# Attention followed by a gated FFN on one core: even 512-column blocks, weights by cast DMA, preps per row, attention a block ahead

## The chip, the cores and the metric

The kernel runs on one core of a Trainium2 chip. The metric is device time in microseconds (us) for one execution; the time before is 392.04 us, the median of three runs (389.96 to 392.66). Engines are named as the profile names them: PE is TensorE's matmul stream and PEld its weight loads, DVE is VectorE, ACT is ScalarE, POOL is GpSimd, and SP is SyncE, which only issues transfers here.

## The reference

The inputs are q, k and v of shape (8 batches, 8 heads, 576 rows, 64), and three FFN weights of shapes 512 x 1536 (gate), 512 x 1536 (value) and 1536 x 512 (out), all float32. The output is 4608 x 512 float32.

```
theta = pi/2 * arange(S) / S                       # S = 576
phi(x) = concat([relu(x) * cos(theta), relu(x) * sin(theta)], axis=-1)
kv  = einsum('bhsf,bhsd->bhfd', phi(k), v)
z   = sum(phi(k), axis=rows)
att = einsum('bhsf,bhfd->bhsd', phi(q), kv) / (phi(q) . z + 1e-6)
x   = att with heads side by side, reshaped to (4608, 512)
out = (gelu(x @ w_gate) * (x @ w_val)) @ w_out
```

So each batch needs two products whose inner size is small (kv with 65 columns, the last being z; nm, the numerator and the denominator), and then every row passes through three dense products, which are most of the arithmetic.

## The kernel before

Everything runs on one core, in an order that is written out by hand: `tc.manual_schedule()` keeps each engine's instructions in the order in which the code names them, and the framework only adds the waits. A loop such as "for jt in range(JT)" below is therefore an order on five queues at once. An instruction that waits holds back everything behind it on its engine.

**Layout.** The 8 heads are 4 pairs (`pair`, NP = 4); a pair fills 128 partitions, 64 per head, and each partition holds R = 9 consecutive rows of 64 values. The 4608 tokens are columns of `xT`; the FFN works on blocks of BLK = 512 columns (9 blocks), while a batch has 576 columns, so batch and block boundaries drift apart. JT = 12 is the number of 128-wide slices of the hidden size 1536; a pass over `jt` for one block is called a block here, and one `jt` of it a slot.

**Attention of one batch.** `prep` (L151) makes qp and kp: per pair and for cosine and sine, one DVE instruction over 128 x 576 values with two tensor sources, the data and the broadcast table. `cast_v` (L187) makes the bfloat16 copy of v with the column of ones, on POOL. `kv_unit` (L237, L245) runs 72 small matmuls and two ACT copies. `turn_q` (L220) turns qp into qT with two DMA transposes on SP; `turn_q_pe` (L205, L212) does it for batch 0 with TensorE transposes and ACT copies. `nm_unit` (L260, L271 to L273) takes 128 columns of qT at a time, five steps per batch (NT = 5): eight matmuls, then three DVE instructions (den, rec, x). `xt_unit` (L309, L317) turns x and ACT copies it into `xT`.

**FFN of one block.** `gv_unit` (L332, L340, L345) does one slot: four matmuls for the gate and four for the value into one PSUM tile `gv_ps` (two buffers), gelu on ACT, the product hT on DVE. A slot's `gv_ps` is free for the slot after next when its hT is done. `o_part` (L370, L379) does the out product of 128 rows; in the steady state a third of it, four matmuls, stands in each slot, for the block before. `flush` (L359) stores the finished rows from SP.

**Loads.** All loads are issued by SP. The weights come in float32 through a staging pool of four buffers in four column slices (L90, L101), and ACT (L96) and POOL (L97, L105) cast them. q, k and v come as two halves per batch and tensor (L71), with three buffers each.

**Order.** Batch 0's loads, then the first two weight slices; batch 0's preps, spread over DVE, ACT (`prep_act`, L166) and POOL (`prep_pool`, L178, L179); kv, then `attend_burst(0)`: all five nm/xt steps with nothing between. Then the gates of batch 0's 576 columns as two halves of 288, with batch 1's preps in the last slots; then kv and the burst of batch 1; then the out product of block 0 by itself; then the segment of 448 columns that completes block 1, in which batch 2's preps, transposes, kv and nm/xt steps are woven; then blocks 2 to 8. In block i, for i from 2 to 6, batch i + 1 is attended: q preps in slots 0 and 1, the transposes and k preps from slot 2, kv in slot 5, nm from slot 6. Blocks 7 and 8 have no attention. The tail is the out product of block 8.

Of the kernel before, what the change touches and what calls it, by code (L numbers as in the profile page):

```python
# [9 lines left out]
FP32 = mybir.dt.float32  # L10
# [6 lines left out]
def kernel(  # L17
# [31 lines left out]
    wst = ctx.enter_context(tc.tile_pool(name="wst", bufs=4))  # L49
    inp = ctx.enter_context(tc.tile_pool(name="inp", bufs=3))  # L50
# [15 lines left out]
    def load(name, src, b, half, pieces=1):  # L66
        t = inp.tile([128, 2, R * D], FP32, name=name)
        view = rows(src, b)
        step = 2 // pieces
        for m in range(0, 2, step):  # L70
            nc.sync.dma_start(  # L71
                out=t[:, m:m + step], in_=view[:, 2 * half + m:2 * half + m + step]
            )
        staged[name, b, half] = t
# [7 lines left out]
    W_SLICES = [(0, 3), (3, 3), (6, 3), (9, 3)]  # L82
    wstage = {}

    def load_w(i):
        jt0, n = W_SLICES[i]
        sl = slice(jt0 * 128, (jt0 + n) * 128)
        for name, src in (("wgf", wg_r), ("wvf", wv_r)):
            t = wst.tile([128, CT, 384], FP32, name=name, tag="w")
            nc.sync.dma_start(out=t[:, :, 0:n * 128], in_=src[:, :, sl])  # L90
            wstage[name, i] = t

    def cast_w(i):
        jt0, n = W_SLICES[i]
        sl = slice(jt0 * 128, (jt0 + n) * 128)
        nc.scalar.copy(wg_sb[:, :, sl], wstage["wgf", i][:, :, 0:n * 128])  # L96
        nc.gpsimd.tensor_copy(wv_sb[:, :, sl], wstage["wvf", i][:, :, 0:n * 128])  # L97

    def load_wo(i):
        t = wst.tile([128, 3, C], FP32, name="wof", tag="w")  # L100
        nc.sync.dma_start(out=t, in_=wo_r[:, 3 * i:3 * i + 3])  # L101
        wstage["wof", i] = t

    def cast_wo(i):
        nc.gpsimd.tensor_copy(wo_sb[:, 3 * i:3 * i + 3], wstage["wof", i])  # L105


    for half in range(2):
        load("qf", q, 0, half, pieces=2)
    for half in range(2):  # L110
        load("kf", k, 0, half, pieces=2)
        load("vf", v, 0, half, pieces=2)
# [33 lines left out]
    def prep(name, b, pair, part, n=1):  # L146
        dst = phi_tile(name, b)
        src = staged[name[0] + "f", b, pair // 2]
        tab = (cos_t, sin_t)[part]
        for m in range(pair, pair + n):  # L150
            nc.vector.scalar_tensor_tensor(  # L151
                dst[:, m, :, part * D:(part + 1) * D],
                src[:, m % 2].rearrange("p (j d) -> p j d", j=R),
                0.0,
                tab[:, :, None].to_broadcast([128, R, D]),
                op0=ALU.max,
                op1=ALU.mult,
            )

    def prep_act(name, b, half, part):  # L160

        dst = phi_tile(name, b)
        src = staged[name[0] + "f", b, half].rearrange("p m (j d) -> p m j d", j=R)
        tab = (cos_t, sin_t)[part]
        for j in range(R):
            nc.scalar.activation(  # L166
                dst[:, 2 * half:2 * half + 2, j, part * D:(part + 1) * D],
                src[:, :, j],
                AF.Relu,
                scale=tab[:, j:j + 1],  # L170
            )

    def prep_pool(name, b, half, part):
        dst = phi_tile(name, b)
# [6 lines left out]
            pos,  # L181
            tab[:, None, :, None].to_broadcast([128, 2, R, D]),
            op=ALU.mult,
        )

    def cast_v(b, half, copy=nc.gpsimd.tensor_copy):
        copy(  # L187
# [335 lines left out]
```

## Time and profile before

| | us |
|---|---|
| median of the runs shown (3) | 392.04 |
| the profiled execution, its own time | 394.85 |
| span of that execution in the trace | 392.7 |

| stage | from | to | length |
|---|---|---|---|
| loads, preps, kv and burst of batch 0 | 0 | 26.4 | 26.4 |
| gates of batch 0, 2 x 288 columns, 12 slots | 26.4 | 62.4 | 36.0 |
| kv and burst of batch 1 | 62.4 | 76.0 | 13.6 |
| out product of block 0 | 76.0 | 88.4 | 12.4 |
| gates of 448 columns, attention of batch 2 | 88.4 | 125.6 | 37.2 |
| blocks 2 to 6, attention of batches 3 to 7 | 125.6 | 315.8 | 190.2 |
| blocks 7 and 8 | 315.8 | 378.0 | 62.2 |
| out product of block 8, last stores | 378.0 | 392.7 | 14.7 |

All times of stages and rows below are those of the one profiled execution, counted from the start of its span; that execution took 0.7% longer than the median. A row of the profile names the line of the code, the engine, the operation, what it writes and reads, and in brackets how long the engine stood idle before it and who released it. "PEclk" is the clock that TensorE was granted, as a share of full speed.

### The profile page before, as it was taken

The numbers are of one execution on the slowest core, as the hardware profiler recorded it, in microseconds if no ns is written. First come the engines' busy times: TensorE is split into PE (matmuls) and PEld (weight loads), VectorE is DVE, ScalarE is ACT, GpSimd is POOL, SyncE is SP. The second block draws the span as 40 slices with busy tenths as digits, with TensorE's granted clock in tenths as the row PEclk, the third lists the DMA queues.
The fourth block names the chain that finished last, engine by engine and source line by source line (L and its number), as shares of the span: only waits on it lengthen the run. The fifth ranks groups of instructions, "written<-read, shape, count | busy, mean of one in ns | idle before, by whom it ended". The sixth has DMA issues, their size and how long they took to land.

```text
span 392.7 us, 6081 instructions
## 1 busy us (share of the span) xinstructions
PE 342.5 (87%) x2484; PEld 177.1 (45%) x2484; DVE 204.6 (52%) x379; ACT 128.7 (33%) x242; POOL 36.8 (9%) x35
## 2 busy tenths in 40 slices
PE   2588955899576988998999999979997999999995
PEld 2365633544243444544544454535443544444442
DVE  6653496504945873587449556915693522222210
ACT  5755421213123331433333242314232333223321
POOL 1821530000202000200020011002000000000000
PEclk9999986599888998999999999989999999999999
DMA  8989908029495099309933990597056111111214
GB/s 265 381 278 362 388 15 120 2 66 357 65 222 214 2 142 321 128 1 126 340 126 44 192 350 6 86 246 258 2 84 118 29 27 42 40 27 28 52 42 95
DMA packets 57467, 55.83 MB, mean 142 GB/s; under 512 B 34912, under 2 KB 39008, under 8 KB 57440
## 3 DMA queue, kind: packets, MB, share of 16 engines
q1 hardware_dynamic: 57440, 55.45, 51.7%
q8 instruction: 19, 0.31, 0.3%
q14 instruction: 8, 0.07, 0.0%
HBM read 37.75 MB, written 9.44 MB: 120 GB/s over the span
## 4 chain that ended last, share of the span: by engine, by line
PE 71%; DMA 14%; DVE 8%; ACT 3%; POOL 2%; issue 1%; ACTq 0%; DVEq 0%; POOLq 0%
PE gv_ps L332 41%; PE o_ps L370 17%; PE gv_ps L370 6%; DVE qp L151 4%; PE xt L309 3%; PE nm L260 3%; DMA qT_1449<-qp 2%; DMA qT_3175<-qp 2%; DMA qT_2744<-qp 2%; DMA qT_1113<-qp 2%; DMA qT_702<-qp 2%; DMA qT_1881<-qp 2%; DVE hT L345 2%; DMA qT_2312<-qp 2%; DVE x_sb L273 1%; POOL pos L178 1%
## 5 line engine op out<-in xcount | busy, mean ns | idle before, releaser
L345 DVE TENSOR_TENSOR hT<-gel,gv_ps 128x512 bf16<-128x512 f32 (+2 forms) x132 | 76.0, 589 | 152.2 <-ACT gel L340 152.0
L340 ACT ACTIVATE gel<-gv_ps 128x512 f32<-128x512 f32 (+2 forms) x120 | 66.5, 555 | 203.9 <-PE gv_ps L332 203.0
L332 PE MATMUL gv_ps<-xT,wg_sb 128*128 128x512 bf16 x336 | 88.7, 388 | 0.0
L332 PE MATMUL gv_ps<-xT,wv_sb 128*128 128x512 bf16 x336 | 87.5, 383 | 0.0
L370 PE MATMUL o_ps<-wo_sb,hT 128*128 128x512 bf16 x336 | 87.1, 382 | 0.0
L332 PEld LDWEIGHTS <-wg_sb 128*128 128x128 bf16 x480 | 47.6, 101 | 64.0 <-issue 18.0
L332 PEld LDWEIGHTS <-wv_sb 128*128 128x128 bf16 x480 | 48.6, 101 | 49.9 <-issue 4.2
L370 PEld LDWEIGHTS <-hT 128*128 128x128 bf16 x432 | 41.2, 100 | 44.7 <-issue 3.5
L332 PE MATMUL gv_ps<-xT_335,wg_sb 128*128 128x288 bf16 (+1 forms) x144 | 30.0, 335 | 11.2 <-DVE hT L345 10.9
L332 PE MATMUL gv_ps<-xT_335,wv_sb 128*128 128x288 bf16 (+1 forms) x144 | 30.3, 339 | 0.0
L151 DVE SCALAR_TENSOR_TENSOR qp<-qf,cos_t 128x576 bf16<-128x576 f32 x32 | 26.0, 849 | 2.5 <-DMA qf<-in_q_dram 2.4
L151 DVE SCALAR_TENSOR_TENSOR kp<-kf,cos_t 128x576 bf16<-128x576 f32 x32 | 25.9, 851 | 1.5 <-DMA kf<-in_k_dram 1.5
L273 DVE TENSOR_TENSOR x_sb<-nm,rec 128x512 bf16<-128x512 f32 x34 | 23.5, 692 | 1.2
L370 PE MATMUL gv_ps<-wo_sb,hT 128*128 128x512 bf16 x96 | 23.3, 407 | 0.0
L151 DVE SCALAR_TENSOR_TENSOR kp<-kf,sin_t 128x576 bf16<-128x576 f32 x30 | 22.3, 788 | 0.0
L151 DVE SCALAR_TENSOR_TENSOR qp<-qf,sin_t 128x576 bf16<-128x576 f32 x30 | 21.4, 752 | 0.0
L309 PE MATMUL xt<-ident,x_sb 128*128 128x128 bf16 x144 | 15.6, 238 | 4.2 <-DVE x_sb L273 3.2
L187 POOL CAST vx_132<-vf 128x1152 bf16<-128x1152 f32 x7 | 8.7, 1250 | 112.1 <-DMA vf<-in_v_dram 77.9
L379 ACT COPY o_sb<-o_ps 128x512 f32<-128x512 f32 x28 | 16.4, 586 | 7.4 <-PE o_ps L370 7.4
L187 POOL CAST vx_134<-vf 128x1152 bf16<-128x1152 f32 x8 | 9.2, 1150 | 102.0 <-DMA vf<-in_v_dram 102.0
L317 ACT COPY xT<-xt 128x512 bf16<-128x512 bf16 (+1 forms) x34 | 16.7, 501 | 4.8 <-PE xt L309 4.7
L237 PEld LDWEIGHTS <-kp 64*128 64x128 bf16 x576 | 11.0, 100 | 9.7 <-issue 4.0
(77 smaller groups left out, 171.9 us busy)
## 6 DMA issues: line engine op xcount, KB each, us to landing
out_dram<-o_sb SPq DMA_DIRECT2D x72, 128.0 KB, 2.4
qf<-in_q_dram SPq DMA_DIRECT2D x14, 576.0 KB, 5.0
kf<-in_k_dram SPq DMA_DIRECT2D x14, 576.0 KB, 7.2
vf<-in_v_dram SPq DMA_DIRECT2D x14, 576.0 KB, 9.7
wgf<-in_moe_w_gate_dram SPq DMA_DIRECT2D x4, 768.0 KB, 6.6
wvf<-in_moe_w_val_dram SPq DMA_DIRECT2D x4, 768.0 KB, 7.8
wof<-in_moe_w_out_dram SPq DMA_DIRECT2D x4, 768.0 KB, 12.6
qf<-in_q_dram SPq DMA_DIRECT2D x4, 288.0 KB, 4.1
```

The costliest lines, as they stand in the source:

```text
L151: nc.vector.scalar_tensor_tensor(dst[:, m, :, part * D:(part + 1) * D], src[:, m % 2].rearrange("p (j d) -> p j d", j=R), 0.0, tab[:, :, N ...
L187: copy(vx_tiles[b % 2][:, 2 * half:2 * half + 2, :, 0:D], staged["vf", b, half].rearrange("p m (j d) -> p m j d", j=R),)
L237: nc.tensor.matmul(ps[:, i, pair * (D + 1):(pair + 1) * (D + 1)], lhsT=kp[rr, pair, j, :], rhs=vx[rr, pair, j, :], start=(j == 0), stop=(j ...
L260: nc.tensor.matmul(ps[:, h // 4, (h % 4) * (D + 1):(h % 4 + 1) * (D + 1)], lhsT=qT[b][h % 2][:, h // 2, c0:c0 + 128], rhs=kv_sb[b][:, h // ...
L273: nc.vector.tensor_tensor(x, nm[:, :, :, 0:D], rec[:, :, :, None].to_broadcast([128, 2, 4, D]), op=ALU.mult,)
L309: nc.tensor.transpose(out=ps[:, ct, :], in_=x[:, ct * 128:(ct + 1) * 128], identity=ident)
L317: nc.scalar.copy(xt[:, :, base + c:base + c + m], ps[:, :, o:o + m])
L332: nc.tensor.matmul(ps[:, 0:n], lhsT=w[:, ct, js], rhs=xt[:, ct, cc:cc + n], start=(ct == 0), stop=(ct == CT - 1),)
L340: nc.scalar.activation(gel[:, 0:n], g_ps[:, 0:n], AF.Gelu)
L345: nc.vector.tensor_mul(hT[hb][:, jt, c:c + m], gel[:, o:o + m], v_ps[:, o:o + m])
L370: nc.tensor.matmul(o_ps[i], lhsT=hT[blk][:, jt, tt * 128:(tt + 1) * 128], rhs=wo_sb[:, jt, :], start=(jt == 0), stop=(jt == JT - 1),)
L379: nc.scalar.copy(o_sb, o_ps.pop(i))
```

## The change

**Blocks.** The first gate pass no longer covers a batch's 576 columns in two halves of 288. Block 0 has its own 512 columns (the first four slots as twice 256, so that they can start when two nm/xt steps of batch 0 are done), then come the 64 columns that batch 0 still has, in block 1, then the 448 columns that complete block 1. hT and xT have one tile per block.

**Weights.** The staging pool and the casts on ACT and POOL are gone. POOL issues transfers that cast from float32 to bfloat16 on the way into `wg_sb`, `wv_sb` and `wo_sb`, in column groups of 1, 2, 3, 3 and 3 slices of 128, and `w_out` in two halves. A one-column copy (`probe`) that reads the second half of batch 0's k stands ahead of them on POOL. q of batch 1 stands between the weight loads, k and v of batch 1 behind the last gate group and ahead of `w_out`.

**Loads of q, k, v.** One tile per tensor and batch in place of two halves, and one buffer in place of three. Batch 0 comes from SP in the order q, k, v; later batches come from POOL.

**Preps.** Per row j and for cosine and sine, one DVE instruction over four pairs (128 x 256 values) with one tensor source and the table's column as a per-partition scalar, 36 per batch for q and k, in place of 16 instructions of 128 x 576 with two tensor sources. `prep_act` and `prep_pool` are gone.

**Turning q.** Batches 1 and 2 are turned by TensorE as well, three rows at a time. For batches 3 to 7 the preps of q stand in slots 9 to 11 of the block before, with the DMA transposes at its end.

**Weaving.** Batch 0's last nm/xt steps stand between the first gate slots. Batch 1's k preps, kv and nm/xt steps stand in the 64-column pass. The out product of block 0 is woven into the 448-column pass. kv's copy out of PSUM is one instruction (two for batch 0).

```diff
-    wst = ctx.enter_context(tc.tile_pool(name="wst", bufs=4))
-    inp = ctx.enter_context(tc.tile_pool(name="inp", bufs=3))
+    inp = ctx.enter_context(tc.tile_pool(name="inp", bufs=1))
...
+    def load(eng, name, src, b, cuts=((0, 4),)):
+        t = inp.tile([128, NP, R * D], FP32, name=name)
+        for m, n in cuts:
+            eng.dma_start(out=t[:, m:m + n], in_=rows(src, b)[:, m:m + n])
+        staged[name, b] = t
...
+    def load_w(jt0, n):
         sl = slice(jt0 * 128, (jt0 + n) * 128)
+        nc.gpsimd.dma_start(out=wg_sb[:, :, sl], in_=wg_r[:, :, sl])
+        nc.gpsimd.dma_start(out=wv_sb[:, :, sl], in_=wv_r[:, :, sl])
+
+    def load_wo(jt0, n):
+        nc.gpsimd.dma_start(out=wo_sb[:, jt0:jt0 + n], in_=wo_r[:, jt0:jt0 + n])
+
+    load(nc.sync, "qf", q, 0, ((0, 1), (1, 1), (2, 2)))
+    load(nc.sync, "kf", k, 0, ((0, 2), (2, 2)))
+    load(nc.sync, "vf", v, 0, ((0, 2), (2, 1), (3, 1)))
...
+    def prep(name, b, j0, j1, m=0, n=NP):
...
+        src = staged[name[0] + "f", b].rearrange("p m (j d) -> p m j d", j=R)
+        for j in range(j0, j1):
+            for part, tab in enumerate((cos_t, sin_t)):
+                nc.vector.tensor_scalar(
+                    dst[:, m:m + n, j, part * D:(part + 1) * D],
+                    src[:, m:m + n, j],
+                    0.0,
+                    tab[:, j:j + 1],
+                    op0=ALU.max,
+                    op1=ALU.mult,
+                )
...
+    probe = consts.tile([128, 1], FP32)
+    nc.gpsimd.tensor_copy(probe, staged["kf", 0][:, 2, 0:1])
+    load_w(0, 1)
+    load_w(1, 2)
+    load_w(3, 3)
+    load(nc.gpsimd, "qf", q, 1)
+    load_w(6, 3)
+    load_w(9, 3)
+    load(nc.gpsimd, "kf", k, 1)
+    load(nc.gpsimd, "vf", v, 1)
+    load_wo(0, 6)
+    load_wo(6, 6)
+
+    prep("qp", 0, 0, 4, 0, 2)
+    prep("qp", 0, 0, 4, 2, 2)
+    turn_q_pe(0, 0, 4, pool=True)
+    prep("kp", 0, 0, R, 0, 2)
+    prep("kp", 0, 0, R, 2, 2)
+    for m, n in ((0, 2), (2, 1), (3, 1)):
+        cast_v(0, m, n, nc.scalar.copy)
+    kv_unit(0, 2)
+    nm_unit(0, 0)
+    nm_unit(0, 1, True)
+    xt_unit(0, 0)
+    xt_unit(0, 1, True)
+    prep("qp", 0, 4, 8)
+    gv_unit(0, 256, 0)
+    turn_q_pe(0, 4, 4)
+    gv_unit(0, 256, 1)
+    prep("qp", 0, 8, R)
+    nm_unit(0, 2)
+    gv_unit(0, 256, 2)
+    xt_unit(0, 2)
+    nm_unit(0, 3)
+    gv_unit(0, 256, 3)
+    xt_unit(0, 3)
+    turn_q_pe(0, 8, 1)
+    for jt in range(4):
+        gv_unit(256, 256, jt)
+        if jt == 0:
+            nm_unit(0, 4)
+        if jt == 1:
+            xt_unit(0, 4)
+    for jt in range(4, JT):
+        gv_unit(0, BLK, jt)
+        if jt in (5, 6, 7):
+            prep("qp", 1, 3 * (jt - 5), 3 * (jt - 4))
+        if jt in (7, 9, 11):
+            turn_q_pe(1, 3 * ((jt - 7) // 2), 3)
     for jt in range(JT):
+        gv_unit(BLK, S - BLK, jt)
+        if jt in (0, 2, 4):
+            prep("kp", 1, 3 * (jt // 2), 3 * (jt // 2) + 3)
+        if jt in (3, 4, 5, 6):
+            cast_v(1, jt - 3, 1, (nc.scalar.copy, nc.gpsimd.tensor_copy)[jt % 2])
+        if jt == 7:
+            kv_unit(1)
+            load_batch(2)
+        if jt >= 8:
+            nm_unit(1, jt - 8, jt % 2)
+        if jt >= 9:
+            xt_unit(1, jt - 9, jt % 2)
+    nm_unit(1, 4)
+    xt_unit(1, 3)
+    xt_unit(1, 4)
...
+    for jt in range(JT):
+        gv_unit(S, 2 * BLK - S, jt)
+        if jt in (3, 4, 5):
+            prep_step("qp", 2, jt - 3)
+        if jt in (5, 6, 7):
+            turn_q_pe(2, 3 * (jt - 5), 3)
+        if jt in (6, 7, 8):
+            prep_step("kp", 2, jt - 6)
+        if jt in (7, 8):
+            cast_v(2, 2 * jt - 14, 2)
         if jt == 9:
+            kv_unit(2)
+        if jt >= 10:
+            nm_unit(2, jt - 10)
+            if jt == 10:
+                load_batch(3)
+        if jt >= 3:
+            o_step(0, jt - 3)
+    xt_unit(2, 0)
+    for t in range(2, NT):
+        nm_unit(2, t)
+        xt_unit(2, t - 1)
+        o_step(0, 7 + t)
+    xt_unit(2, NT - 1)
+    for i in range(3):
+        prep_step("qp", 3, i)
+    turn_q(3, 0, NP)
+
+    for blk in range(2, 9):
+        b = blk + 1
         for jt in range(JT):
+            gv_unit(BLK * blk, BLK, jt)
             if b < B:
+                if jt < 3:
+                    prep_step("kp", b, jt)
+                if 1 <= jt < 5:
+                    cast_v(b, jt - 1, 1)
+                if jt == 5:
+                    kv_unit(b)
                     if b + 1 < B:
                         load_batch(b + 1)
+                if 6 <= jt < 6 + NT:
+                    nm_unit(b, jt - 6)
+                if jt >= 7:
+                    xt_unit(b, jt - 7)
+                if b + 1 < B and jt >= 9:
+                    prep_step("qp", b + 1, jt - 9)
+                    if jt == 11:
+                        turn_q(b + 1, 0, NP)
+            o_step(blk - 1, jt)
```

Here `load_batch(b)` loads q, k and v of a batch from POOL, `prep_step(name, b, i)` preps rows 3i to 3i + 2, and `o_step(blk, i)` is the i-th third of an out product, four matmuls.

## The prediction

> **What bounds the kernel now.** I read the chain of waits first, then busy time by stage, then the waits, then one block in order of time. The chain, by engine:
>
> ```profile
> PE 71%; DMA 14%; DVE 8%; ACT 3%; POOL 2%; issue 1%; ACTq 0%; DVEq 0%; POOLq 0%
> ```
>
> TensorE carries it, with 14% on transfers and 8% on VectorE. Stages (length, then busy us of PE, PEld, DVE, ACT, POOL, granted clock, DMA share, GB/s):
>
> ```profile
> 0.00:26.40 26.40, 13.10 (x168) 10.00 (x169) 18.10 (x30) 14.46 (x28) 11.67 (x15) 1.00 0.95 322
> ...
> 62.40:76.00 13.60, 7.60 (x134) 6.14 (x134) 8.31 (x21) 3.47 (x8) 0.00 (x0) 0.63 0.40 58
> 76.00:88.40 12.40, 12.40 (x49) 5.15 (x47) 0.00 (x0) 2.13 (x4) 0.00 (x0) 0.83 0.23 53
> ...
> 277.30:315.80 38.50, 35.99 (x281) 17.98 (x280) 23.84 (x44) 13.04 (x26) 0.00 (x0) 1.00 0.34 59
> 315.80:346.90 31.10, 31.10 (x146) 14.10 (x144) 8.05 (x13) 9.52 (x16) 0.00 (x0) 1.00 0.15 34
> ```
>
> A block without attention takes 31.1 us, all TensorE. One with attention takes 38.5 here; the five from 125.6 to 315.8 average 38.04. Around one of them:
>
> ```profile
> 296.76 0.19 PE L260 MATMUL nm<-kv_sb,qT_3174 128*128 128x65 bf16 x1
> ...
> 299.46 0.20 PE L260 MATMUL nm<-kv_sb,qT_3175 128*128 128x65 bf16 x1 [2.50 <-DMA qT_3175<-qp]
> ...
> 299.90 0.17 DVE L271 TENSOR_SCALAR den<-nm 128x8 f32<-128x8 f32 x1 [1.61 <-PE nm L260]
> ...
> 302.55 0.39 PE L309 MATMUL xt<-ident,x_sb 128*128 128x128 bf16 x4
> ```
>
> TensorE stands for the second q transpose by DMA, issued four slots (2.6 us each) earlier and 8.7 us under way. Without waits the block would be 12 slots of 2.59 (31.1), a kv product of 1.26, and five nm/xt steps at 0.48 (0.26 nm, 0.22 xt; that slot begins its nm at 302.29 and its o work at 302.77): 34.8. So 3.3 us per block are waits and their clock after-effects.
>
> **The change, part by part**, on the profiled run's clock.
>
> *Blocks 2 to 6.* q preps and both transposes move to the slots before the block. The second lands about 3.4 (first issue) + 8.7 = 12.1 us after the last prep; it is needed at slot 6, some 17 us later, and 5 us of margin remain. SP's stores stand behind the transposes as before, with four o_sb buffers. Saving 5 x 3.3 = 16.5, less 0.3 per block for queueing on DVE: 15.0. Block 2 adds 1.3: 18 q preps stand in DVE's queue ahead of its first hT.
>
> *Prep cost.* The groups by shape (count, busy us, mean ns of one, idle before):
>
> ```profile
> L345 DVE TENSOR_TENSOR hT<-gel,gv_ps 128x512 bf16<-128x512 f32 x84 | 57.3, 688 | 112.7 <-ACT gel L340 112.7
> ...
> L151 DVE SCALAR_TENSOR_TENSOR qp<-qf,sin_t 128x576 bf16<-128x576 f32 x30 | 21.4, 752 | 0.0
> ...
> L271 DVE TENSOR_SCALAR den<-nm 128x8 f32<-128x8 f32 x34 | 5.5, 161 | 13.4 <-PE nm L260 13.4
> ```
>
> 16 two-source instructions per batch (128x576, 0.665 us apart) become 36 one-source ones of 256 elements. No such row exists. Below: the shortest DVE rows, 0.16 to 0.20 us (den, rec). Above: the line through the hT rows (0.214 at 64, 0.688 at 512 elements, in PSUM) gives 0.42 long, less the 0.07 by which L151 rows overlap: 0.35 apart. I take 0.30, the L151 rate per element (0.665 x 256/576), that row being nearest in kind; 0.15 for the 128-element halves (bounds 0.13 to 0.21). Per batch 36 x 0.30 = 10.8, as now (10.6); a DVE gain is not in the sum.
>
> The Trainium skill ("VectorE: DVE Perf Modes", The perf-mode tier table and the errata) says that a one-source fp32 op in SBUF runs two elements per cycle and has a cost of (58 + 128)/0.96 = 194 ns here, an estimate. By it the sum would be 5.5 us less. No run here shows it yet.
>
> *Prologue.* q pieces land at 3.6, about 4.4 and 6.7 (DVE waits 0.25 there). k now precedes v: before, the tenth piece of 288 KB landed at 11.28 and the fourth at 6.7, 0.76 each, so k lands at 8.2 and 9.8, v's halves at 11.3 and about 14 beside the first weights. DVE: 36 k preps of 0.15 from 8.2 end at 13.6. ACT: q copies of 1024 (1.0 each, scaled from 0.65 for 576) end by 11.1, v casts 1.19 + 0.65 x 2 end at 14.7. kv's second half (1.06) then runs to 15.9, copy to 16.5; from there the 4.2 us that two nm/xt steps took (19.70 to 23.9) give the first gate matmul at 21.0 instead of 26.4. Bounds 19 to 24.
>
> *Block 0, 256-wide start.* Four slots twice, with the transposes of rows 4 to 8 and three nm chains in series. TensorE starts at half rate (four 288-column matmuls take 0.95 at 26.46, 0.49 from 29.6), so slot 0 ends at 21.0 + 1.7 and 16 transposes at 24.7; ACT (gelu's table load of 1.28 is over by then) copies qT until 26.9; nm follows. DVE does hT, the last preps and the den, rec, x chain (1.25 with hand-overs): x at 29.8. The next step waits for that x, its own at 31.9; the third waits for row 8's transposes and copies as well, x at 35.3; two slots of 0.87 and the turn of xt remain: end 37.5, where 8 x 0.87 = 7.0 would be bare TensorE work. Bounds 34 to 41, by how far each chain overlaps the slots between.
>
> *Rest of block 0.* 8 x 1.73 + 36 transposes at 0.055 = 15.8. In slots 5 to 7 DVE holds 6 x 0.30 + 0.69 = 2.5 against 1.73, and only 0.2 of slack without o work: +2.1. End 55.4.
>
> *The 64-column remainder.* TensorE needs 7 us, but DVE sets the pace: 18 preps (5.4), 8 hT at 0.214, hand-overs: 8.5; kv cold 2.0 and copy 0.8; then five steps at 1.05 plus four hT, with ends, 8.2. Together 19.5: end 74.9. Before, gates of batch 0 and attention of batch 1 were done at 76.0: the head alone wins almost nothing up to here.
>
> *The 448 columns.* Before: 12.4 of bare o work, then 37.2. After: gates 12 x 1.51 = 18.2, nine o steps 7.8, 36 transposes 2.0, kv 1.26, nm 0.6, cold start 1.5: 31.4; then 6.8 for four steps at 1.65 (121.91 to 123.56), three o steps inside. End 113.1 instead of 125.6.
>
> *Loads.* ACT and POOL lose all weight casts (4 x 1.47 on ACT, 8 x 1.48 on POOL). The loads go from SP to POOL's queue, behind a probe that waits for k's second half (9.8); v casts on POOL stand behind every issue. POOL issues nothing in this trace. An issue costs between the 0.37 of a weight load and the 3.4 to 4.6 of a transpose on SP; I take 0.5, and at 4 the ninth column group would come at about 54 instead of 47, +7. Due: 8.1 MB by 47, 12.0 MB (to the first half of w_out) by 79; so 220 GB/s hides everything, and the first five slices moved 265 to 388. A cast transfer has no row; I take the plain rate, 240 or more, cost zero. Input pools with one buffer: a load waits for the last prep of its tile, three slots earlier, cost zero with 10 us in hand.
>
> The Trainium skill ("SBUF — State Buffer", SBUF: two separate sides) speaks against this: transfers issued from GpSimd starve for descriptors while VectorE runs two-port ops, which the new preps could be. If the first weights waited for the prologue's last prep, they would come at 13.6 + 6.6 (landing row of wgf) = 20.2, just in time for 21.0; each later burst of preps would cost at most its own length. No run here shows it.
>
> *Unchanged*: blocks 7 and 8 (62.2), tail (14.7).
>
> Sum: 113.1 + 5 x 34.8 + 1.3 + 1.5 + 62.2 + 14.7 = 366.8 of span, against 392.7. The execution took 394.85, 2.15 more than its span, and 0.7% more than the median of 392.04. So 368.9 in its terms, 366 in the median's.
>
> **Rivals.**
>
> *Preps at the lower row, 0.20 (0.13)*: prologue -0.7, block 0 -1.7, remainder -1.8, block 2 -1.3: 361. For it: one source, no broadcast operand. Against: no row.
>
> *Preps at 0.35 (0.21)*: +1.0, +1.0, +0.9, +0.9; slots 9 and 10 hold 3.85 against 3.07 and the following four 2.8 against 2.6, 2.4 of backlog against 2.0 of slack, inside the 0.3 per block: 370. Part of my range.
>
> *The woven order does not take*: transposes or q loads land late behind the load queue, blocks stay at 38.0: 366 + 15 = 381. For it: transposes already take 6 to 9 us and share engines with 3.5 MB of loads per batch. Against: loads start at slot 5, the transposes at slot 11.
>
> *Slower: the load queue sets the pace.* Place: w_out's first half, due at 79. It decides where the delay passes 26 us, so when 12.0 MB take 96 us: below 125 GB/s. At 100 GB/s it lands at 130, +50: 416; at 110, 405. For it: casts and POOL issue are unseen, and the narrow first columns make 512-byte runs. Against: the present queue at 322 GB/s in the first stage, with weight rows of 1536 bytes.
>
> **How the numbers follow.** Forecast with the dearer preps 0.57, cheap preps 0.16, order not taking 0.10 (a fifth of it with slow issue on top, near no change), load queue slower 0.10, smaller mishaps that eat most of the gain 0.07 (half of them near no change). Faster by over 1% (below 388.1): 0.57 + 0.16 + 0.08 + 0.04 = 0.85. Within 1%: 0.05. Slower: 0.10. One per cent is about what a measurement of this kernel can tell from no change. Range: below, 361 less 6 for a shorter remainder and 256-wide start (chains overlapping more than I followed): 355. Above, 381 plus part of a slow issue: 384.
>
> **What would show it.** Right: no DMA wait on nm in blocks 2 to 6, each about 35 us; first gate matmul near 21; block 2 starting near 113; no wait of gate matmuls for weights. The mean of the new prep row decides between 361 and 370. Wrong: gate or o matmuls released by weight DMAs; blocks still at 38 with a new releaser, DVE or the q load; the 64-column stage much longer than 20.

## The result and the profile after

The changed kernel takes 406.98 us (median of four runs, 402.82 to 410.67) against 392.35 for the kernel before beside it (389.96 to 394.16). The ratio is 1.034, with a 95% interval of 1.023 to 1.045: it is slower, where 366 was forecast. Its profiled execution has a span of 405.9 us.

First the chain of waits of the changed kernel by engine, which answers to the "PE 71%; DMA 14%" of before:

```profile
PE 64%; DMA 23%; DVE 9%; ACT 2%; issue 1%; SPq 0%; ACTq 0%
```

Transfers carry 23% of the chain where they carried 14%. The stages say where. The first column is the stretch in us from the span's start, then its length and the busy time of PE, PEld, DVE, ACT and POOL, the granted clock, the DMA share and the GB/s:

```profile
0.00:22.80 22.80, 8.87 (x113) 5.64 (x114) 15.18 (x67) 7.89 (x13) 5.96 (x17) 1.00 1.00 225
22.80:38.80 16.00, 12.80 (x120) 10.14 (x120) 7.03 (x21) 7.84 (x15) 6.89 (x9) 1.00 0.54 122
38.80:55.40 16.60, 16.28 (x108) 8.57 (x108) 10.22 (x27) 8.65 (x14) 2.00 (x3) 1.00 1.19 276
55.40:72.80 17.40, 11.01 (x221) 9.75 (x221) 11.75 (x46) 7.36 (x22) 1.70 (x3) 0.71 0.63 217
72.80:109.30 36.50, 34.97 (x312) 19.30 (x311) 22.29 (x65) 16.19 (x28) 6.78 (x9) 1.00 0.38 120
109.30:328.40 219.10, 182.32 (x1385) 90.40 (x1383) 111.64 (x315) 61.61 (x114) 19.20 (x28) 0.91 0.61 117
```

The first five rows are everything ahead of block 2. It starts at 109.3, and before it started at 125.6: the head won 16 us. The last row is blocks 2 to 6. They take 219.1, 43.8 each, and took 190.2 (first row below): 29 us lost. TensorE is busy for 182 of the 219, so the rest is standing still, at a mean clock of 0.91.

```profile
125.60:315.80 190.20, 180.70 (x1384) 89.31 (x1382) 116.87 (x215) 61.68 (x118) 9.88 (x9) 0.98 0.53 134
```

The waits of nm steps for a transpose (total, times, longest, in us), the three longest of before and then all of the changed kernel's:

```profile
PE nm L260 <- DMA qT_1449<-qp: 2.6, 1, 2.6
PE nm L260 <- DMA qT_2744<-qp: 2.6, 1, 2.6
PE nm L260 <- DMA qT_3175<-qp: 2.5, 1, 2.5
```

```profile
PE nm L217 <- DMA qT_1562<-qp: 14.9, 1, 14.9
PE nm L217 <- DMA qT_2894<-qp: 14.5, 1, 14.5
PE nm L217 <- DMA qT_2001<-qp: 5.7, 1, 5.7
PE nm L217 <- DMA qT_2447<-qp: 1.7, 1, 1.7
```

Each time it is the second q transpose of a batch, as before, but for 36.8 us in all where seven waits made 13.0 (9.5 of it in blocks 2 to 6). Their place in time, for batch 6, from the timelines of SP, of POOL and of PE (start, length, and in brackets the idle time before and who ended it):

```profile
243.63 3.30 SPq L178 DMA_TRANSPOSE qT_2893<-qp  x1
247.03 9.93 SPq L178 DMA_TRANSPOSE qT_2894<-qp  x1
```

```profile
244.51 0.85 POOL L68 DMA_DIRECT2D qf<-in_q_dram  x1 [12.49 <-DVE qp L129]
251.59 0.75 POOL L68 DMA_DIRECT2D kf<-in_k_dram  x1 [6.23 <-DVE kp L129]
252.34 0.75 POOL L68 DMA_DIRECT2D vf<-in_v_dram  x1
```

```profile
259.93 0.19 PE L217 MATMUL nm<-kv_sb,qT_2893 128*128 128x65 bf16 x1
274.67 0.24 PE L217 MATMUL nm<-kv_sb,qT_2894 128*128 128x65 bf16 x1 [14.55 <-DMA qT_2894<-qp]
```

The code names POOL's loads of the next batch in slot 5, behind kv. For batch 7 POOL issues q at 244.51, less than a microsecond after the first transpose of batch 6, and k and v before the block's kv, which TensorE begins at 256.06. Nothing on POOL waits for slot 5: its queue runs ahead until it meets a wait, and the wait it meets is the single input buffer. DVE's last q prep frees q's buffer, and the same prep releases the transposes; the last k prep frees k's. So POOL fires its loads at the transposes. The second transpose, issued at 247.03, lands 27.6 us later.

The pairs of batches 3 to 6, which have loads beside them, land after 10.3 to 10.6 us (first) and 25.6, 18.8, 14.7 and 27.6 us (second). Batch 7's pair has no load beside it: 6.7 and 6.5. Before, the second ones of blocks 2 to 6 took 6.1 to 8.8. Counted from the first issue to the second landing, the four pairs take 29.2, 22.1, 18.1 and 31.0 us, and nm stood for 14.9, 5.7, 1.7 and 14.5 of it: a pair may take 16.4 to 16.5, in block 2 14.3, before it costs anything.

### The profile page after: what moved, and what is told of

Same layout as the page of the kernel before. It is cut to its first block, busy times and chain, and to the rows that moved or that the text cites. A ratio compares the mean times of both kernels' runs of the same rounds, so it can differ in the third digit from the quotient of the medians.

```text
span 405.9 us, 6421 instructions
## 1 busy us (share of the span) xinstructions
PE 338.9 (83%) x2588; PEld 176.5 (43%) x2588; DVE 195.0 (48%) x561; ACT 131.5 (32%) x240; POOL 42.5 (10%) x68
## 4 chain that ended last, share of the span: by engine, by line
PE 64%; DMA 23%; DVE 9%; ACT 2%; issue 1%; SPq 0%; ACTq 0%
PE gv_ps L282 38%; PE o_ps L315 17%; DMA qT_2894<-qp 7%; DMA qT_1562<-qp 6%; DMA qT_2001<-qp 5%; DMA qT_2447<-qp 4%; DVE kp L129 4%; PE nm L217 3%; PE gv_ps L315 3%; DVE x_sb L230 2%; PE xt L261 2%; DMA qf<-in_q_dram 1%; PE nm L198 1%; PE nm L162 1%; DVE hT L293 1%; ACT gel L290 1%
## 5 line engine op out<-in xcount | busy, mean ns | idle before, releaser
L293 DVE TENSOR_TENSOR hT<-gel,gv_ps 128x512 bf16<-128x512 f32 (+3 forms) x124 | 76.2, 617 | 149.9 <-ACT gel L290 149.9
L290 ACT ACTIVATE gel<-gv_ps 128x512 f32<-128x512 f32 (+3 forms) x124 | 67.2, 543 | 221.6 <-PE gv_ps L282 220.7
L282 PE MATMUL gv_ps<-xT,wg_sb 128*128 128x512 bf16 (+3 forms) x496 | 118.1, 363 | 5.5 <-DVE hT L293 4.3
L282 PE MATMUL gv_ps<-xT,wv_sb 128*128 128x512 bf16 (+3 forms) x496 | 117.1, 361 | 0.0
L315 PE MATMUL o_ps<-wo_sb,hT 128*128 128x512 bf16 x384 | 101.2, 387 | 0.0
L129 DVE TENSOR_SCALAR kp<-kf,sin_t 128x256 bf16<-128x256 f32 (+1 forms) x81 | 28.2, 348 | 0.0
L129 DVE TENSOR_SCALAR kp<-kf,cos_t 128x256 bf16<-128x256 f32 (+1 forms) x81 | 28.2, 348 | 0.0
L129 DVE TENSOR_SCALAR qp<-qf,cos_t 128x256 bf16<-128x256 f32 (+1 forms) x76 | 25.8, 339 | 4.5 <-DMA qf<-in_q_dram 4.5
L230 DVE TENSOR_TENSOR x_sb<-nm,rec 128x512 bf16<-128x512 f32 x37 | 25.6, 691 | 1.3
L129 DVE TENSOR_SCALAR qp<-qf,sin_t 128x256 bf16<-128x256 f32 (+1 forms) x76 | 25.8, 340 | 0.0
L324 ACT COPY o_sb<-o_ps 128x512 f32<-128x512 f32 x32 | 18.8, 587 | 8.9 <-PE o_ps L315 8.9
L261 PE MATMUL xt<-ident,x_sb 128*128 128x128 bf16 x148 | 14.5, 221 | 4.4 <-DVE x_sb L230 3.5
L217 PE MATMUL nm<-kv_sb,qT_1562 128*128 128x65 bf16 x20 | 2.1, 204 | 14.9 <-DMA qT_1562<-qp 14.9
L261 PEld LDWEIGHTS <-x_sb 128*128 128x128 bf16 x160 | 10.3, 100 | 9.4 <-DVE x_sb L230 8.0
L217 PE MATMUL nm<-kv_sb,qT_2894 128*128 128x65 bf16 x20 | 2.1, 204 | 14.5 <-DMA qT_2894<-qp 14.5
## 6 DMA issues: line engine op xcount, KB each, us to landing
qf<-in_q_dram POOLq DMA_DIRECT2D x7, 1152.0 KB, 10.5
```

The lines of the kernel that those rows point to most:

```text
L129: nc.vector.tensor_scalar(dst[:, m:m + n, j, part * D:(part + 1) * D], src[:, m:m + n, j], 0.0, tab[:, j:j + 1], op0=ALU.max, op1=ALU.mult,)
L217: nc.tensor.matmul(ps[:, h // 4, (h % 4) * (D + 1):(h % 4 + 1) * (D + 1)], lhsT=qT[b][h % 2][:, h // 2, c0:c0 + 128], rhs=kv_sb[b][:, h // ...
L230: nc.vector.tensor_tensor(x, nm[:, :, :, 0:D], rec[:, :, :, None].to_broadcast([128, 2, 4, D]), op=ALU.mult,)
L261: nc.tensor.transpose(out=ps[:, ct, :], in_=x[:, ct * 128:(ct + 1) * 128], identity=ident)
L282: nc.tensor.matmul(ps[:, 0:n], lhsT=w[:, ct, js], rhs=xt[:, ct, cc:cc + n], start=(ct == 0), stop=(ct == CT - 1),)
L290: nc.scalar.activation(gel[:, 0:n], g_ps[:, 0:n], AF.Gelu)
```

## The experiments

The times are medians, the ratio in brackets is to the kernel before in the same session, with its interval. "Crawl" is a count made from the DMA records: the 1 us slices between 100 and 310 us in which the transposes' 256-byte packets take over 100 ns in the mean (usually 18 to 30) while packets of a load run beside them.

| kernel: what lies beside the transposes | pair takes | second lands | nm waits for it | crawl | us |
|---|---|---|---|---|---|
| changed kernel: q, then k and v, from POOL | 18.1–31.0 | 14.7–27.6 | 36.8 | 20 | 406.98 |
| e1: nothing, POOL gated | 10.1–11.4 | 6.5–8.0 | 0 | 0 | 364.06 |
| e2: nothing, loads on SP | 9.9–11.6 | 6.3–8.0 | 0 | 0 | 363.36 |
| e5: as changed, two buffers | 11.5–30.9 | 8.1–27.4 | 30.7 | 17 | 406.66 |
| e10: as changed, loads in short rows | 18.1–24.4 | 14.7–21.0 | 18.2 | 2 | 386.22 |
| e6: q alone from POOL | 12.3–18.3 | 8.8–14.8 | 3.9 | 8 | 370.03 |
| e14: k and v from POOL, q later | 10.1–12.8 | 6.4–9.2 | 0 | 0 | 363.02 |
| e13: q from POOL, then k, v from ACT, in one pair; behind the transposes in three | 14.0–23.2 | 10.2–19.7 | 8.9 | 4 | 379.04 |
| e12: q and k at once, from POOL | 16.3–17.0 | 12.8–13.4 | 2.2 | 0 | 369.63 |
| e11: q and k at once, from ACT | 13.1–16.2 | 6.0–8.1 | 0 | 0 | 365.19 |
| e4: q from ACT, k 6.5 to 7.7 later | 14.0–17.4 | 7.9–11.4 | 1.2 | 0 | 366.62 |
| e9: q and k, v too or later, from ACT | 15.7–19.2 | 8.2–12.7 | 1.6 | 0 | 396.27 |

The rows give the pairs of batches 3 to 6, beside which the changed kernel loads batches 4 to 7. "Pair takes" counts from the first issue to the second landing, "second lands" from the second's own issue. The texts below call it a collapse when second transposes land after 14 us and more.

**Is it the overlap? (e1, e2.)** e1 makes POOL wait until both transposes have landed; e2 moves the loads to SP's queue, where they stand behind the transposes.

```diff
 # e1, ahead of load_batch(b + 1) in slot 5
+                        for i in range(2):
+                            nc.gpsimd.tensor_copy(probe, qT[b][i][:, NP - 1, 0:1])
 # e2, in load_batch
+        eng = nc.sync if b >= 4 else nc.gpsimd
...
```

> Two one-column copies on POOL that read both halves of qT stand ahead of the loads in slot 5, so that POOL's loads of the next batch can start only when the transposes of this one have landed. Collision theory (loads and transposes in flight together slow each other): transposes land in 6.5 to 9 us, no nm waits for them, blocks 2 to 6 take about 35 us each instead of 43.8, span about 362 to 366, time about 364. Single-buffer theory (one input buffer makes the loads, and so the preps and transposes, late): the gate makes loads later still, so 405 or more. POOL theory (transfers issued by POOL slow SP's transposes by themselves): also about 364, since the two no longer overlap.

> Loads of batches 4 to 7 are issued by SP at the same place of the code (slot 5), so that SP's own order puts them behind the transposes. Collision theory: 362 to 368, blocks of 35 us, transposes 6.5 to 9 us. Single-buffer theory: 400 or more. POOL theory: 362 to 368.

e1 took 364.06 (0.924 [0.919, 0.929]), e2 363.36 (0.922 [0.917, 0.926]). No nm step waits for a transpose in either. One gate on one engine returns 43 us, so the overlap is the whole loss, and what the forecast summed is there.

**A buffer more (e5).** `inp` with `bufs=2`, nothing else.

> The input pool gets two buffers instead of one; nothing else. Collision theory: a q load is still released by the end of the q preps of two batches before, the moment at which a pair of transposes is issued, so transposes stay slow and the time stays at 385 to 407. Single-buffer theory: loads land long before use, 362 to 368. POOL theory: as the collision theory.

406.66 (1.021 [1.012, 1.031]). With two buffers POOL's loads run one batch further ahead, still released by a q prep: q at 116.41, 165.88 and 202.81, each within 0.9 us of a pair's first issue. So three pairs collide as before, and batch 6's pair (6.1 and 8.1) has no load left beside it. A second buffer alone does not keep POOL off the transposes.

**Is it only the transposes that suffer? (e3.)** POOL's loads as in the changed kernel, batches 3 to 7 turned by TensorE.

```diff
-    turn_q(3, 0, NP)
...
+                if 1 <= jt < 4:
+                    turn_q_pe(b, 3 * (jt - 1), 3)
...
-                    if jt == 11:
-                        turn_q(b + 1, 0, NP)
```

> All POOL loads stay as in the changed kernel; batches 3 to 7 are turned by TensorE in slots 1 to 3 of their block, so no DMA transpose is left. Theory (all of the loss is in the transposes, and POOL's early loads hurt nothing else): the 364 of the gated kernel plus 36 transposes on TensorE at 0.055, 2.0 us, for each of five batches, so 370 to 376, and blocks 2 to 6 near 37. Rival (early POOL loads also cost VectorE, the stores or TensorE's feed something): blocks 2 to 6 at 40 or more, 385 to 405.

373.71 (0.948 [0.944, 0.953]). A window of the length of its blocks 2 to 6 (it begins 1 us before block 2), in which TensorE never stands:

```profile
107.80:292.80 185.00, 184.86 (x1566) 98.38 (x1565) 112.04 (x315) 84.14 (x145) 19.24 (x28) 1.00 0.34 106
```

From block 2's first gate matmul (108.75) to block 7's (293.08) it is 36.9 us per block. Early POOL loads cost the rest of the kernel nothing that shows; the 10 us over e1 agree with the 2.0 us of TensorE transposes per batch that were expected.

**Any load, or POOL's? (e4, e9, e11, e12.)** e4 issues q, k and v of batches 4 to 7 from ACT in slots 0, 3 and 5.

> Loads of batches 4 to 7 are issued by ACT, close to the moments at which POOL now issues them: q in slot 0 right behind the last q prep, k in slot 3, v in slot 5. No load of these batches comes from POOL. Collision theory: transposes still take 10 us and more (second ones 14 to 28 us), blocks 2 to 5 stay above 38 us, time 385 to 407. POOL theory: transposes 6.5 to 9 us, time about 364. Single-buffer theory: as now, about 405.

366.62 (0.931 [0.926, 0.938]). The theory that any load beside a transpose ruins it fell: no second transpose took over 11.4 us, although q ran beside the first and k beside the second in all four pairs (k issued at 154.49 and landed at 163.95, the second transpose from 152.63 to 163.49). But v started while the second was under way in one pair only. e9 put all three in slot 0, with two buffers (the expectation takes q alone to have run beside the transposes in e4; k had too):

> Two input buffers, and q, k and v of batches 4 to 7 all issued by ACT in slot 0 of the block, so that 3.5 MB on a hardware queue start at the same time as the transposes; in the earlier ACT kernel the trace shows only q truly beside them, since k went out 7.7 us after the first transpose. Theory (the collapse to 14.7 to 27.6 us needs POOL's software queue): the transposes share the engines with 3.5 MB at 300 GB/s, 12 us, and land within 8 to 16 us; DMA waits of nm under 8 us in all; 365 to 376. Rival (it is the amount in flight, on any queue): second transposes at 18 us or more, as in the changed kernel, and 385 to 410.

396.27 (1.011 [1.007, 1.015]): the time is the rival's, but the landings, 8.2 to 12.7, are the theory's. The timeline of ACT in e9 shows what else took the time:

```profile
152.02 0.47 ACTq L68 DMA_DIRECT2D kf<-in_k_dram  x1
162.31 0.37 ACTq L68 DMA_DIRECT2D vf<-in_v_dram  x1
162.78 1.09 ACT L290 ACTIVATE gel<-gv_ps 128x512 f32<-128x512 f32 x2 [10.69 <-DMA qT<-qp]
```

The third issue stood on ACT until the first transpose of the pair landed (issued 151.91, landed 162.2), and the gelus behind it stood too. In the trace that transpose and v's load count on the same semaphore, which the framework hands out again; in three of the four batches this cost 10.6 to 11.5 us. An issue on a compute engine holds up its computing for whatever it waits for. It also means that v was beside both transposes in one batch only (landings 11.8 and 8.2 there) and beside the second alone in the other three, from the first's landing on. So e9 settles nothing by its time; by its landings, three loads on ACT's queue made no collapse.

e11 and e12 remove that: two buffers, v from SP in slot 5, and q and k issued together at the moment of the transposes, from ACT or from POOL.

```diff
 # slot 0 of blocks 2 to 5, e11 with nc.scalar and without the first line
+                    nc.gpsimd.tensor_copy(probe, phi["qp", b][:, NP - 1, R - 1, F - 1:F])
+                    load(nc.gpsimd, "qf", q, b + 1)
+                    load(nc.gpsimd, "kf", k, b + 1)
...
```

> Two input buffers; for batches 4 to 7 q and k are issued by ACT in slot 0 of the block, beside the two transposes, and v by SP in slot 5, behind them. 2.3 MB on a hardware queue then lie beside the transposes, without the third issue on ACT that stood 10.7 us in the run before. Theory (POOL's software queue is needed for the collapse): transposes land within 8 to 13 us, DMA waits of nm under 2 us in all, 364 to 369. Rival (amount alone, any queue): second transposes at 14 us or more and 375 or more.

> The same as the run beside it, with q and k issued by POOL in place of ACT, released by a one-column copy that reads the last prep of q, so at the moment at which the transposes are issued. Same bytes, same buffers, same place of v; only the queue differs. Theory (POOL's software queue is needed): second transposes at 14 to 26 us, DMA waits of nm over 10 us in all, 378 to 405. Rival (amount alone): landings and time as in the run beside it, within 3 us.

e11: 365.19 (0.931 [0.925, 0.938]); e12: 369.63 (0.942 [0.935, 0.949]). The same 2.3 MB cost 4.4 us more on POOL's queue than on ACT's, and a pair takes 16.3 to 17.0 in place of 13.1 to 16.2. (In e11 the second transpose is itself issued 7 to 8 us after the first, so its own landing flatters it. The moments are not quite the same either: ACT issues q 0.3 us ahead of the first transpose, in the first pair 2.4, and POOL 0.5 behind it.) But e12 was expected at 378 to 405: both fell short of a collapse. In these four runs loads beside the transposes delay a pair by 3 to 9 us, on either queue, which the margin nearly covers; the collapse to 31 needs something more.

**Which of POOL's loads? (e6, e13, e14.)** e6 leaves q early on POOL and holds k and v behind the transposes; e13 leaves q early on POOL and issues k and v from ACT in slot 3; e14 issues q from SP in slot 5 and leaves k and v on POOL, early, as in the changed kernel. This is the whole edit of e14 against the changed kernel:

```diff
-                        load_batch(b + 1)
+                        load(nc.sync, "qf", q, b + 1)
+                        load(nc.gpsimd, "kf", k, b + 1)
+                        load(nc.gpsimd, "vf", v, b + 1)
```

> Batches 4 to 7: q is loaded from POOL as early as in the changed kernel (when q's preps release the buffer), k and v are held back until both transposes have landed. 1.15 MB then lies beside the transposes, less than the 2.3 MB of q and k that ACT's queue carried beside them at little cost. Theory (POOL's software queue is what the transposes can't stand, whatever the amount): the second transpose of a pair still lands 12 to 25 us after its issue, and the time is 375 to 400. Rival (it is the amount in flight, q, k and v at once): the transposes land within 8 to 11 us, no DMA wait of nm over 1 us, and the time is 364 to 368.

> One input buffer; q of batches 4 to 7 from POOL as early as in the changed kernel, k and v from ACT in slot 3, at about the moment (8 us after the first transpose's issue) at which POOL issues them in the changed kernel. Theory (the collapse needs transfers of POOL's queue that start while the second transpose is under way): no collapse, transposes as in the run with q alone early, 9 to 15 us, 366 to 372. Rival (anything that starts in the middle of the second transpose, on any queue): second transposes at 15 to 27 us, 385 to 407. If an issue on ACT waits for a transpose to land, the time is longer by that wait, and the landings alone decide.

> One input buffer; k and v of batches 4 to 7 from POOL as early as in the changed kernel (released by the last k prep, 8 us after the first transpose's issue), q from SP in slot 5, behind the transposes. Theory (k and v from POOL in the middle of the second transpose make the collapse): q no longer delays the transposes, so they are nearly done when k and v start; if they are still under way the second lands at 14 us or more and the time is 375 to 405. Rival (q's early transfer is needed too, since it alone makes the transposes late enough to meet k and v): landings of 6 to 9, 363 to 367.

e6: 370.03 (0.940 [0.934, 0.946]), between the two expectations: a late transpose, a small wait. e13: 379.04 (0.965 [0.958, 0.972]), between the theory's 366 to 372 and the rival's 385 to 407. ACT's issues of k and v in its first two pairs:

```profile
120.64 0.43 ACTq L68 DMA_DIRECT2D kf<-in_k_dram  x1
121.24 0.55 ACTq L68 DMA_DIRECT2D vf<-in_v_dram  x1
...
169.53 0.41 ACTq L68 DMA_DIRECT2D kf<-in_k_dram  x1
171.29 0.40 ACTq L68 DMA_DIRECT2D vf<-in_v_dram  x1
```

In the second pair the transposes landed at 169.46 and 171.22: k stood until the first had landed and v until the second had, on semaphores that they share with the transposes, as in e9. It was so in three of the four pairs (14.0 to 14.2), and in each a gelu stood 6.7 to 6.9 us behind these issues. So only the first pair tests the queue. There k and v start within 0.3 us of the moments of the changed kernel (120.7 and 121.5), and the second transpose takes 19.7 and the pair 23.2, against 25.6 and 29.2: a collapse, within the 15 to 27 that the rival gave for any queue.

e14: 363.02 (0.922 [0.918, 0.927]), the fastest of all, beside e2. In e14's chain and in its window for blocks 2 to 6 the transfers are gone:

```profile
PE 82%; DVE 11%; ACT 3%; DMA 2%; issue 1%; SPq 0%; ACTq 0%
```

```profile
109.80:284.00 174.20, 172.35 (x1358) 88.09 (x1381) 110.87 (x314) 61.50 (x114) 15.99 (x24) 1.00 0.57 147
```

34.8 us per block, clock 1.00. The loss takes two steps. q's load, fired at the transposes, makes the pair late: 12.3 to 18.3 us when it is alone (e6), in place of 10. So the second transpose is still under way when k and v come 7 to 8 us after the first issue, and the pair stretches to 18 to 31. Without the first step (e14) the transposes are almost done by then, and the same early k and v cost nothing. That k and v have to come from POOL for it is not shown: the one pair that tests it (e13) collapses with ACT's. What the second step is, in packets by 2 us in the changed kernel's DMA records:

```
from us   transposes (256 B packets)       POOL's loads (4.6 KB packets)
244       704, mean  27 ns                 none
246      1088, mean  30 ns                 none
248       512, mean  29 ns                  63, mean 273 ns
250      none                              141, mean 220 ns
252       431, mean  96 ns                  49, mean 191 ns
254       938, mean  30 ns                   8, mean 568 ns
256       144, mean 228 ns                  11, mean 178 ns
258       189, mean 190 ns                  13, mean 781 ns
260       207, mean 151 ns                   9, mean 188 ns
262       150, mean 229 ns                  12, mean 603 ns
264       158, mean 190 ns                  30, mean 1061 ns
```

From 256 on the transposes move 37 to 53 KB in 2 us, where they moved 180 to 280, and the loads 41 to 138 where alone they moved 650 (row 250), while the packets' time still fills the engines (a DMA share of 1.03 to 1.97 in these rows). Both are slower together than either alone. In e13's first pair the milder form of it, two slices at 111 and 120 ns, stands beside ACT's loads alone: POOL's q had landed at 124.5.

**Shorter rows (e10).** POOL's loads in two transfers each, of 1024 and 1280 bytes per row.

> POOL's loads of batches 2 to 7 cut into two transfers each, of 1024 and 1280 bytes per row in place of 2304; in the trace POOL's packets are 4.6 KB, ACT's 2.3 KB, the transposes' 0.25 KB. Theory A (a short transpose packet waits behind a long load packet): with packets about half as long the second transposes land within 10 to 15 us and the time is 370 to 388. Theory B (it is the software queue itself, by its descriptors, not the length of its packets): twice as many descriptors, so the transposes land no sooner than the 14.7 to 27.6 of the changed kernel, and the time is 400 to 425.

386.22 (0.982 [0.974, 0.990]), inside theory A's range, with the crawl down from 20 slices to 2; but the second transposes still land at 14.7 to 21.0, which theory A put at 10 to 15. And the change is not the one that the expectation assumes: by the DMA records POOL's packets are 4.1 and 5.1 KB, four short rows each where they held two of 2304 bytes, and as many as before (256 per tensor). So packet length was not varied. Shorter rows in twice as many transfers take 20 us off; which of the two does it, and how, is not shown.

**One part of the change alone (e7).** The kernel before, with q, k and v of batches 3 to 7 from POOL.

```diff
-            nc.sync.dma_start(
+            (nc.gpsimd if b >= 3 else nc.sync).dma_start(
```

> The kernel before, with one part of the change alone: q, k and v of batches 3 to 7 are loaded from POOL instead of SP. Theory (POOL's transfers beside transposes are enough, no other part of the change is needed): the second transpose lands 12 us or more after its issue, blocks 2 to 6 lengthen by 5 to 13 us each, and the time is 415 to 460. Rival (the margin or the weave of the changed kernel matters, the queue alone does not): transposes at 6 to 9 as in the kernel before, 390 to 397.

435.19 (426.08 to 438.14; the profile is of the fastest), against 393.98. From one batch's first transpose to the next it is 43.2 to 44.5 us, where a block took 38.0, and the nm waits for transposes go from 13.0 to 38.0, although a pair takes only 15.7 to 16.5, without any crawl beside a load. Before, a pair took 10.5 to 12.3 and nm already stood for it, so every microsecond counted. The time was expected; the 12 us or more for the second were not reached in blocks 2 to 6 (11.1 to 11.5).

**The preps by themselves (e8).** e2 with the same 36 instructions per batch, but two tensor sources.

```diff
-                nc.vector.tensor_scalar(
+                nc.vector.scalar_tensor_tensor(
...
-                    tab[:, j:j + 1],
+                    tab[:, j:j + 1, None].to_broadcast([128, n, D]),
```

> The kernel whose batch loads come from SP (363.4), with the preps made again with two tensor sources (the data and the broadcast table), in the same 36 instructions of 256 elements per batch and tensor pair at the same places. Theory (one-source form doubles the rate per element, but VectorE is not what bounds): rows of 256 elements become some 0.33 apart instead of 0.26, 2.5 us of VectorE per batch, mostly hidden; prologue +1, the rest +0 to +3, so 364 to 368. Rival (the preps are what sets blocks 2 to 6): 5 times 2.5 and the prologue on top, 375 to 380.

369.93 (0.939 [0.934, 0.944]), 6.6 above e2: dearer than the 1 to 5 of the theory, far from the rival's 12 and more. By the spans, 2.4 of it falls ahead of block 2 and 2.9 in the five blocks. The groups by shape (total us, mean ns of one), of e8 and then of e2:

```profile
L129 DVE SCALAR_TENSOR_TENSOR kp<-kf,cos_t 128x256 bf16<-128x256 f32 x63 | 27.0, 428 | 0.0
```

```profile
L129 DVE TENSOR_SCALAR kp<-kf,cos_t 128x256 bf16<-128x256 f32 x63 | 21.9, 347 | 0.0
```

They start 0.335 apart in e8 and 0.262 apart in e2; the instructions of 128 elements start 0.20 apart in both.

## Why the prediction was wrong

**The step that failed.** "The second lands about 3.4 (first issue) + 8.7 = 12.1 us after the last prep; it is needed at slot 6, some 17 us later, and 5 us of margin remain", and its defence against the rival: "loads start at slot 5, the transposes at slot 11". The slot where the code names a load is no time on a queue that nothing ties to the slots. The same text had noted that "a load waits for the last prep of its tile" and put it at "cost zero with 10 us in hand"; that wait was not a cost but the trigger. It releases the load at the very moment at which the same prep releases the transposes. By the changed kernel's own records a pair took 18.1 to 31.0 where 12.1 was summed; the 17 that it may take was nearly right (16.5, and 14.3 in block 2), and all four pairs went beyond it. The 8.7 came from the kernel before, in which the loads stand behind the transposes on SP (in blocks 2 to 6 none was issued over 2.1 us ahead of a pair's landing), so that its landings were measured with almost nothing beside them.

**The rivals.** "The order does not take" named transposes that land late behind the load queue, and gave 381 because it took the old 38.0 per block as its worst. The mechanism was right and the bound was not: a block can get worse than before, 43.8. "The load queue sets the pace" did not occur: no matmul waited for a weight.

**The other terms held**, each stage ahead of block 2 within 2.1 us; a late start was made up by shorter stages behind it. Beside the forecast stand the changed kernel and e14:

| stage | forecast | changed | e14 |
|---|---|---|---|
| first gate matmul at | 21.0 | 22.8 | |
| block 0, 256-wide start | 16.5 | 16.0 | |
| rest of block 0 | 17.9 | 16.6 | |
| 64-column remainder | 19.5 | 17.4 | |
| 448 columns and burst | 38.2 | 36.5 | |
| block 2 starts at | 113.1 | 109.3 | 109.8 |
| blocks 2 to 6 | 176.8 | 219.1 | 174.2 |
| the rest | 76.9 | 77.5 | 77.3 |
| span | 366.8 | 405.9 | 361.3 |

So -3.8 in the head, +42.3 in the blocks, +0.6 behind them make the 39.1 between 366.8 and 405.9. Of the 44.9 us between the blocks of the changed kernel and of e14, 36.8 are the waits themselves; the remainder goes with a granted clock of 0.91 instead of 1.00.

**The preps.** 0.30 was taken for a row, and 0.262 was measured, between the two bounds. That it came so near is partly luck: a rate per element was carried over without a fixed part, and the same scaling gave 0.15 for 128 elements, where 0.196 was measured. The one-source form does run at twice the rate at the margin, as the Trainium skill says ("VectorE: DVE Perf Modes", The perf-mode tier table): from 128 to 256 elements the spacing grows by 0.066 us, 0.52 ns per element, and by 0.135, 1.05 ns per element, with two sources. The whole cost that the prediction worked out from the page, 194 ns for 256 elements, is too low: 262 apart and 347 long. The page itself says below the row of 58 cycles (in its section on the errata) that the row falls short and some 150 were measured, by which the estimate would have been 290 ns.

**The first gate matmul, 1.8 late.** The k preps of the prologue took 8.1 us in the changed kernel where 5.4 were taken: 0.196 apart instead of 0.15, and slower beside POOL's issues. They began at 9.3 in place of 8.2, behind the q preps, and ended at 17.4, so that they, and not v's casts (14.7 in the forecast), were the last to reach kv. Part of VectorE's timeline of e2, in which POOL issues weights from 11.76 on:

```profile
11.81 0.28 DVE L129 TENSOR_SCALAR kp<-kf,sin_t 128x128 bf16<-128x128 f32 x1
...
15.70 0.27 DVE L129 TENSOR_SCALAR kp<-kf,sin_t 128x128 bf16<-128x128 f32 x1
15.88 0.56 DVE L129 TENSOR_SCALAR kp<-kf,cos_t 128x128 bf16<-128x128 f32 x1
16.08 0.43 DVE L129 TENSOR_SCALAR kp<-kf,sin_t 128x128 bf16<-128x128 f32 x1
```

**The rule that spoke against the change.** The Trainium skill ("SBUF — State Buffer", SBUF: two separate sides) says that VectorE and GpSimd lock each other out of a shared port. It was weighed as a stall of the weights until the prologue's last prep. In the changed kernel it is an alternation like the one above. In e8, with two sources, it is the full stall, on POOL's timeline:

```profile
11.24 5.99 POOL L338 COPY probe<-kf 128x1 f32<-128x1 f32 x1 [9.35 <-DMA kf<-in_k_dram]
17.17 0.90 POOL L80 DMA_DIRECT2D wg_sb<-in_moe_w_gate_dram  x1
```

A copy of one column stood for 5.99 us, until the last k prep (16.88, 0.30 long) was done, and the first weight load behind it. The first gate matmul was not later for it (22.6, against 23.5 in e2), so the stall was hidden, as the prediction's estimate by that page had it.

**What stays open.** Why the transposes' packets take 150 to 230 ns in some stretches beside loads is not shown. In every pair that collapsed, q came from POOL by itself at the moment of the transposes (the changed kernel, e5, e6, e10, e13), and no run with q and k on ACT's queue collapsed (e4, e9, e11). But POOL's queue is not enough, since e12 has no crawl with q and k at once, and k and v need not be POOL's, since e13's first pair collapsed with ACT's. Only one pair shows the latter, and no run has q from ACT with k and v from POOL in the middle of the second transpose. Which property of the loads it is (queue, packets, rows, or their order in time) stays open; that it is their overlap with the transposes does not.

## What to carry to other kernels

When a load moves to another queue, ask what will release it there: on a queue that runs ahead, it is the buffer, not the place in the code, and the release of that buffer can come at the very moment of the next step's own transfers, as it did here. A landing time holds only for what ran beside it where it was measured. Where one transfer is on the path and another has slack, put them on one queue in that order (e2), or move the one load that fires at the same moment (e14); both give 363, 7.8% below the kernel before.

## What the runs showed of the hardware

- DMA transposes on SP's queue beside POOL's transfers can make both crawl: 256-byte packets at 150 to 230 ns in place of 18 to 30, a second transpose at up to 27.6 us in place of 6.5. With q and k on ACT's queue no second transpose took over 12.7 us (e4, e9, e11), and no such slice was found; with q on POOL's and k and v on ACT's, the one pair that overlapped took 19.7, with slices at 111 and 120 ns (e13).
- An issue from POOL takes 0.75 to 0.92 us on its timeline in the changed kernel (0.5 had been taken), one from ACT 0.37 to 0.55 (e4, e9, e11, e13).
- A one-source instruction lets POOL in between two of its kind, at the price of 0.36 to 0.60 us for some in place of 0.28 (changed kernel, e2); with two sources POOL's small copy stood for 5.99 us, through a whole run of them (e8).
